# A fused linear attention and feed-forward kernel: one batch's x transposed by DMA instead of TensorE, and the steps of three batches set at other places

## The chip, the cores and the metric

The kernel runs on one core of a Trainium2 chip. The core has five engines, each with its own in-order instruction stream: TensorE (PE in the profile; PEld is its weight load), VectorE (DVE), ScalarE (ACT), GpSimd (POOL) and SyncE (SP). Here SP does nothing but issue DMA transfers; one transfer of the whole program is issued by ACT. The engines wait for each other and for transfers through semaphores. The metric is the device time of one execution in microseconds (us), the median of several runs; lower is better.

## The reference

There are 8 batches of 8 heads with 576 positions and head dimension 64. A linear attention with cosine weights is followed by a feed-forward network over all 4608 tokens of width 512.

```python
r = np.maximum(x, 0.0)
phi = np.concatenate([r * cos_w, r * sin_w], axis=-1)     # 64 -> 128 features, for q and k
kv  = np.einsum('bhsf,bhsd->bhfd', k_p, v)
z   = np.sum(k_p, axis=2)
num = np.einsum('bhsf,bhfd->bhsd', q_p, kv)
den = np.einsum('bhsf,bhf->bhs', q_p, z)[..., None] + 1e-06
x   = (num / den).transpose(0, 2, 1, 3).reshape(B * S, H * D)
h   = x @ w_in                                            # 512 -> 2048
out = np.maximum(0.01 * h, h) @ w_out                     # 2048 -> 512
```

## The kernel before

**Tiling.** Of each batch the first 512 positions form one group of tokens, numbered as the batch, 0 to 7. The 64 positions left over of all eight batches form a ninth group, 8. A group's 512 tokens lie as 128 partitions times J = 4 (`p j` with p outer), so one j is a tile of 128 tokens. Everything that TensorE reads is float16, and it accumulates in float32 in PSUM.

**What one batch b needs, in order.**

- `load_k`, `load_v` and `load_main("q")` (L86, with the small tails of k and v at L96) fetch the inputs as float32. Each of them takes a buffer from the pool `stage`, which has seven.
- `kv_steps` puts `k_tail` and four `k_main` (both halves of phi of k, L226 on DVE, L224 on ACT), two `v_main` and one `v_tail` (casts of v to float16, L232 on ACT or L234 on DVE; `v_tail` is two instructions, one for each half of the partitions), then `kv_all` (L290 for the tails, which come first and read `vtail`; L299 for the main part) and the copy of the result to `kv[b]` (L306, on ACT).
- `q_steps` puts four `q_prep` (phi of q, L226 on DVE) and, after every second of them, one `q_transpose_dma` (L342), a DMA transposition of two tiles of phi(q) from SBUF to SBUF, issued by SP.
- `num(b, j)` (L373) multiplies tile j by `kv[b]`. It uses the pool `ps_n`, a single PSUM buffer. `divide` (L384 to L389, on DVE) divides by the denominator into the tile `xs`.
- x must be transposed into `xT` before the first matrix multiplication. For batches 3 to 8 `out_steps` does it with one `x_transpose_dma` (L354) for all four tiles, issued by SP. For batch 2 `x_transpose(2, j)` does it on TensorE, four transposes for each j into a PSUM tile `ps_xt` (L438), which ACT copies to `xT` (L439). Batches 0 and 1 are worked by steps of their own, which are written out by hand.

**The feed-forward part.** `ffn1(g, m)`, short f1(g,m), is four matmuls of 512 columns (L452). Two neighbouring m share a PSUM tile of a pool with two buffers, and ACT applies the leaky ReLU to the pair (L460). `ffn2(g, i)`, short f2(g,i), is four matmuls too (L475); four of them make one output tile of 128 tokens. `ffn2_out` copies it to one of four buffers `osb` (L234 or L232) and stores it (L489).

**The order.** The program order is written by hand: every engine takes its instructions in the order in which the Python code names them. For the main part there is a list `units` of f1 and f2 steps, each with a position; group g's second product and group g+1's first product share the positions 16g to 16g+16. `ahead` says how many f2 steps of the group come before the mixing starts. `at(pos, f, ...)` puts any other step at a position, and `weave` merges the two lists: a step stands ahead of the first unit whose position is not below its own.

**SP's queue.** All transfers but one stand in SP's single queue, in program order. Each also waits until the transfer eight places before it has landed, because the transfers use eight semaphores in turn. A transfer whose source is not ready holds up everything that stands behind it.

Of the kernel before, what the change touches and what calls it, by code (L numbers as in the profile page):

```python
# [9 lines left out]
dt = mybir.dt  # L10
# [3 lines left out]
P = 128  # L14
J = 4
# [3 lines left out]
def kernel(  # L19
# [14 lines left out]
    nc = tc.nc  # L34
# [8 lines left out]
    NKC = DM // P  # L43
# [28 lines left out]
    def psum(where, shape, dtype, name):  # L72
        p = {"h": ps_h, "o": ps_o, "n": ps_n}[where]
        return p.tile(shape, dtype, name=name, tag="ps_" + where)

    st = {}
    ACT, DVE, POOL = nc.scalar, nc.vector, nc.gpsimd
# [96 lines left out]
    ident = const.tile([P, P], dt.float16, name="ident")  # L174
# [55 lines left out]
    def copy(eng, o, i):  # L230
        if eng is ACT:
            nc.scalar.copy(o, i)  # L232
        else:
            eng.tensor_copy(o, i)  # L234
# [112 lines left out]
    def xT_tile(g):  # L347
        if ("xT", g) not in st:
            st["xT", g] = xtpool.tile([P, J, NKC, P], dt.float16, name="xT")
        return st["xT", g]  # L350
# [80 lines left out]
                ps.rearrange("p c (o t) -> p o c t", o=2),  # L431
            )

    def x_transpose(g, j, where="o"):
        xs = st["xs", g][:, j]
        ps = psum(where, [P, NKC, P], dt.float16, "ps_xt")
        for c in range(NKC):
            nc.tensor.transpose(ps[:, c, :], xs[:, 2 * c : 2 * c + 2, :], ident)  # L438
        nc.scalar.copy(xT_tile(g)[:, j], ps)  # L439

    def ffn1(g, m, lo=0, hi=MAIN, chunks=range(NKC), where="h"):
# [18 lines left out]
    def ffn2(g, i, eng=DVE):  # L462
        tt, part = divmod(i, 4)
        if g == NG - 1 and tt == 3:
            last_tile(*divmod(part, 2))
            return
        if part == 0 and ("ps_o", g, tt) not in st:
            st["ps_o", g, tt] = psum("o", [P, DM], dt.float32, "ps_o")
        ffn2_mm(g, tt, 4 * part, 4 * part + 4)
        if part == 3 and eng is not None:  # L470
            ffn2_out(g, tt, eng)

    def ffn2_mm(g, tt, lo, hi):
        for m in range(lo, hi):
# [5 lines left out]
                stop=(m == NFT - 1),  # L480
            )

    def ffn2_out(g, tt, eng):
        ps = st["ps_o", g, tt]
        osb = opool.tile([P, DM], dt.float32, name="osb", tag="osb")
        if g < B:
            copy(eng, osb, ps)
            rows = out[g * S : g * S + MAIN, :].rearrange("(p j) d -> p j d", j=J)
            nc.sync.dma_start(rows[:, tt, :], osb)  # L489
            return  # L490
        copy(eng, osb, ps)
        for o in range(2):
            r0 = (2 * tt + o) * S + MAIN
            nc.sync.dma_start(out[r0 : r0 + TAIL, :], osb[o * TAIL : (o + 1) * TAIL, :])
# [66 lines left out]
    ps = psum("h", [P, 2, 512], dt.float32, "ps_numh")  # L561
# [44 lines left out]
    def f1(g, m, where="h"):  # L606
        return lambda: ffn1(g, m, where=where)

    def f2(g, i):
        return lambda: ffn2(g, i)  # L610
# [3 lines left out]
    def at(pos, f, *args):  # L614
        steps.append((pos, lambda: f(*args)))
# [22 lines left out]
    ps = psum("n", [P, 2, DM], dt.float32, "ps_o")  # L638
# [16 lines left out]
    v_main(1, 6, 8, ACT)  # L655
    ffn2(0, 15, None)
    ffn2_out(0, 2, ACT)
    ffn2_out(0, 3, ACT)
    ffn2(0, 3, None)
    ffn2_mm(0, 1, 12, 14)  # L660
    kv_half(1, 1, "h")
    ffn2_mm(0, 1, 14, 15)
    ps = psum("h", [P, 2, MAIN], dt.float16, "ps_x")
# [24 lines left out]
    for m in range(6, NFT):  # L688
        units.append((8 + m / 2, f1(1, m)))
    for g in range(1, NG):  # L690
        ahead = {1: 8, 2: 4}.get(g, 0)
        order = [f2(g, i) for i in range(ahead)]
        for i in range(16):
            if g + 1 < NG:
                order.append(f1(g + 1, i))
            if ahead + i < 16:
                order.append(f2(g, ahead + i))
        for n, u in enumerate(order):
            units.append((16 * g + 16 * n / len(order), u))
# [3 lines left out]
    def kv_steps(b, start, step, mm, eng_v, n_act=0):  # L703
        at(start - 0.01, kp_tiles, b)
        at(start, k_tail, b, DVE, DVE)
        for i in range(J):
            at(start + (i + 1) * step, k_main, b, i, ACT if i < n_act else DVE, DVE)
        v0, dv = (start + 1.5 * step, 1) if b > 3 else (start + 3 * step, 0.1)
        at(v0, v_main, b, 0, 4, eng_v)
        at(v0 + dv, v_main, b, 4, 8, eng_v)  # L710
        at(v0 + 2 * dv, v_tail, b, eng_v)
        at(mm, kv_all, b)

    def load_steps(b, pk, pv, pq):
        at(pk, load_k, b)
        at(pv, load_v, b)
        at(pq, load_main, "q", q, b)

    def out_steps(b, start, step, lag):
        for j in range(J):  # L720
            at(start + j * step, num, b, j)
        at(start + (J - 1) * step + lag, x_transpose_dma, b)

    def q_steps(b, start, step, lag):
        for j in range(J):
            at(start + j * step, q_prep, b, j)
            if j % 2:
                at(start + j * step + lag, q_transpose_dma, b, j // 2)

    q_steps(2, 8, 0.4, 0.3)  # L730
    kv_steps(2, 9.7, 0.5, 14, DVE, 2)
    for j in range(J):
        at(14.5 + 1.1 * j, num, 2, j)
        at(15.8 + 1.1 * j, x_transpose, 2, j, "o" if j < 2 else "h")

    load_steps(3, 11, 13, 10)
    q_steps(3, 18, 0.8, 0.8)
    kv_steps(3, 20, 0.7, 24, ACT)
    out_steps(3, 24.5, 1.4, 1)

    load_steps(4, 21.4, 22.5, 21.3)
    kv_steps(4, 28, 1.2, 34, ACT)
    q_steps(4, 30, 0.8, 0.8)
    out_steps(4, 36.8, 2, 1.6)

    for b in range(5, NG):
        base = 16 * (b - 2)
# [40 lines left out]
```

## Time and profile before

| | us |
|---|---|
| median of 3 runs | 294.44 (294.29 to 294.61) |
| the profiled execution | 293.82 |
| its span, first to last instruction | 292.0 |
| TensorE's idle time in the span, all waits that the profile names | 1.2 + 0.5 + 0.2 + 0.2 |

The span is what the profile shows; the execution's time has 1.8 us around it. These groups belong to the stages that the change touches (line, engine and operation, output and input, shapes, count, then busy us and the mean ns of one, then the idle time of the engine before them and what ended it):

```profile
L299 PE MATMUL ps_kv<-vmain,kpm 128*128 128x66 f16 x192 | 7.1, 193 | 0.0
...
out_dram<-osb SPq DMA_DIRECT2D x32, 256.0 KB, 2.5
...
qpT<-qp SPq DMA_TRANSPOSE x14, 4.5
...
xT<-xs SPq DMA_TRANSPOSE x6, 4.6
```

The last three are lines on transfers: destination and source, queue, count, KB of each and the median us from issue to landing. A matmul's duration in such a line is from its start to its modelled end. Successive matmuls overlap, so what one costs is the distance between two starts.

### The profile page before, as it was taken

What the parts mean: (1) busy time and instruction counts of PE and PEld (TensorE: products, weight loads), DVE (VectorE), ACT (ScalarE), POOL (GpSimd) and SP (SyncE); (2) the same over time, 40 slices, a digit from 0 to 9 for tenths busy, and PEclk for the clock granted to TensorE, in tenths of its full rate; (3) what the DMA queues carried; (4) which work ended last, traced back from release to release, by engine and by line L of the source; (5) the groups of instructions that cost most, each with busy time, mean ns of one, the idle gap of its engine ahead of it and who ended that gap; (6) DMA issues with size and microseconds to landing.
All of it is one profiled execution on the core that took longest, in us unless ns stands there. A gap on an engine that the chain in (4) does not pass through costs nothing.

```text
span 292.0 us, 4774 instructions
## 1 busy us (share of the span) xinstructions
PE 286.4 (98%) x1958; PEld 152.7 (52%) x1958; DVE 128.7 (44%) x328; ACT 118.4 (41%) x148; POOL 12.7 (4%) x24
## 2 busy tenths in 40 slices
PE   8999999999999999999999999999999999999995
PEld 3585556555555555455545554555445444444444
DVE  6931687926835816823562356333323310000011
ACT  6865266753544632632263226322222222222200
POOL 2264000000000000000000000000000000000000
PEclk9999999999999999999999999999999999999999
DMA  7999999999999999789584989504691051011133
GB/s 233 348 386 407 325 364 335 315 204 324 212 241 318 229 291 298 166 162 338 164 182 84 296 233 199 91 37 110 160 199 38 36 108 38 36 54 54 39 71 73
DMA packets 87909, 56.93 MB, mean 195 GB/s; under 512 B 55888, under 2 KB 80720, under 8 KB 87504
## 3 DMA queue, kind: packets, MB, share of 16 engines
q1 hardware_dynamic: 87808, 56.57, 71.0%
q8 instruction: 15, 0.25, 0.4%
q10 hardware_dynamic: 80, 0.07, 0.1%
q14 instruction: 6, 0.05, 0.1%
HBM read 36.70 MB, written 9.44 MB: 158 GB/s over the span
## 4 chain that ended last, share of the span: by engine, by line
PE 94%; DMA 2%; SPq 1%; ACT 1%; DVE 1%; issue 0%
PE ps_h L452 43%; PE ps_o L475 41%; PE ps_num L373 3%; PE ps_kv L299 2%; DMA vst<-in_v_dram 2%; PE ps_l L504 1%; SPq L96 1%; PE ps_xth L425 1%; PE ps_qt L363 1%; PE ps_numh L409 1%; SPq L86 1%; PE ps_kv L290 0%; PE ps_idle L166 0%; PE ps_kvh L274 0%; ACT qpT L232 0%; PE ps_xt L438 0%
## 5 line engine op out<-in xcount | busy, mean ns | idle before, releaser
L452 PE MATMUL ps_h<-xT,w 128*128 128x512 f16 (+1 forms) x592 | 142.8, 373 | 0.1
L475 PE MATMUL ps_o<-w,g 128*128 128x512 f16 x560 | 139.5, 379 | 0.0
L460 ACT ACTIVATE g<-ps_h 128x1024 f16<-128x1024 f32 x72 | 73.2, 1023 | 128.8 <-PE ps_h L452 128.8
L452 PEld LDWEIGHTS <-w 128*128 128x128 f16 x592 | 64.4, 114 | 52.3 <-issue 0.2
L475 PEld LDWEIGHTS <-g 128*128 128x128 f16 x560 | 54.2, 98 | 61.4
L234 DVE COPY osb<-ps_o 128x512 f32<-128x512 f32 x31 | 21.4, 690 | 77.1 <-PE ps_o L475 75.3
L384 DVE TENSOR_SCALAR den<-ps_num 128x8 f32<-128x8 f32 x28 | 4.6, 165 | 54.9 <-PE ps_num L373 54.9
L389 DVE TENSOR_TENSOR xs<-ps_num,rden 128x512 f16<-128x512 f32 x28 | 19.4, 691 | 1.2 <-DVE rden L388 0.2
L226 DVE TENSOR_SCALAR kpm<-kst,sin_t 128x512 f16<-128x512 f32 (+1 forms) x40 | 16.6, 429 | 1.1 <-DMA kst<-in_k_dram 1.1
L226 DVE TENSOR_SCALAR qp<-qst,cos_t 128x512 f16<-128x512 f32 (+1 forms) x34 | 15.5, 456 | 2.8 <-DMA qst<-in_q_dram 2.8
L226 DVE TENSOR_SCALAR qp<-qst,sin_t 128x512 f16<-128x512 f32 (+1 forms) x34 | 15.5, 456 | 0.0
L373 PEld LDWEIGHTS <-qpT 128*128 128x128 f16 (+1 forms) x256 | 10.6, 101 | 7.3 <-issue 1.7
L232 ACT CAST vmain<-vst 128x1024 f16<-128x1024 f32 (+1 forms) x14 | 12.5, 920 | 2.4 <-DMA vst<-in_v_dram 2.3
L226 DVE TENSOR_SCALAR kpm<-kst,cos_t 128x512 f16<-128x512 f32 (+1 forms) x29 | 13.1, 453 | 0.3 <-DMA kst<-in_k_dram 0.3
L373 PE MATMUL ps_num<-kv,qpT 128*128 128x66 f16 (+1 forms) x256 | 11.8, 194 | 0.0
L166 PE MATMUL ps_idle<-blank 128*128 128x512 f16 x30 | 9.9, 478 | 1.2 <-DVE blank L161 1.2
L234 DVE CAST w<-w2st 128x1024 f16<-128x1024 f32 (+1 forms) x6 | 5.1, 868 | 11.8 <-DMA w2st<-in_moe_w_out_dram 11.8
L232 ACT COPY qpT<-ps_qt 128x1024 f16<-128x1024 f16 x7 | 7.0, 1012 | 5.7 <-PE ps_qt L363 5.7
L234 POOL CAST w<-w1st 128x1024 f16<-128x1024 f32 (+1 forms) x9 | 8.5, 945 | 3.6 <-DMA w1st<-in_moe_w_in_dram 3.6
L388 DVE RECIPROCAL rden<-den 128x8 f32<-128x8 f32 x36 | 7.3, 203 | 1.2
L299 PE MATMUL ps_kv<-vmain,kpm 128*128 128x66 f16 x192 | 7.1, 193 | 0.0
L299 PEld LDWEIGHTS <-kpm 128*128 128x128 f16 x192 | 6.4, 98 | 0.3
(62 smaller groups left out, 99.7 us busy)
## 6 DMA issues: line engine op xcount, KB each, us to landing
out_dram<-osb SPq DMA_DIRECT2D x32, 256.0 KB, 2.5
qst<-in_q_dram SPq DMA_DIRECT2D x7, 1024.0 KB, 6.8
kst<-in_k_dram SPq DMA_DIRECT2D x6, 1024.0 KB, 9.7
vst<-in_v_dram SPq DMA_DIRECT2D x6, 1024.0 KB, 9.4
w1st<-in_moe_w_in_dram SPq DMA_DIRECT2D x7, 512.0 KB, 10.4
w2st<-in_moe_w_out_dram SPq DMA_DIRECT2D x3, 1024.0 KB, 12.9
kst<-in_k_dram SPq DMA_DIRECT2D x4, 512.0 KB, 6.9
vst<-in_v_dram SPq DMA_DIRECT2D x4, 512.0 KB, 7.9
```

The costliest lines, as they stand in the source:

```text
L166: nc.tensor.matmul(ps, lhsT=blank[:, 0:P], rhs=blank)
L226: eng.tensor_scalar(out=o, in0=i, scalar1=0.0, scalar2=col, op0=ALU.max, op1=ALU.mult)
L232: nc.scalar.copy(o, i)
L234: eng.tensor_copy(o, i)
L299: nc.tensor.matmul(ps[:, h % 2, h // 2], lhsT=kpm[:, h, j, :], rhs=vmain[b % 2][:, h, j, :], start=False, stop=(h >= H - 2 and j == J - 1),)
L373: nc.tensor.matmul(ps[lo:hi, h // 4, (h % 4) * NE : (h % 4 + 1) * NE], lhsT=qpT[:, h, lo:hi], rhs=kv[b][:, h, :],)
L384: nc.vector.tensor_scalar_add(den.rearrange("p (a b) -> p a b", a=2), ps[:, :, D : 4 * NE : NE], 1e-6)
L388: nc.vector.reciprocal(rden, den)
L389: nc.vector.tensor_tensor(out=xs, in0=ps[:, :, 0 : 4 * NE].rearrange("p a (b e) -> p a b e", e=NE)[:, :, :, 0:D], in1=rden.rearrange("p (a ...
L452: nc.tensor.matmul(ps[:, m % 2, lo:hi], lhsT=w1[m // 4, c][0][:, w1[m // 4, c][1], m % 4 : 512 : 4], rhs=xT[:, lo // P : hi // P, c, :], s ...
L460: nc.scalar.activation(st["g", g][:, m - 1 : m + 1, :], ps, AF.Lrelu)
L475: nc.tensor.matmul(st["ps_o", g, tt], lhsT=st["g", g][:, m, tt * P : (tt + 1) * P], rhs=w2[:, m, :], start=(m == 0), stop=(m == NFT - 1),)
```

## The change

There are five edits.

1. `x_transpose` is gone. Batch 2 uses `out_steps(2, 14.4, 0.9, 0.8)`: its four `num` stand 0.9 of a position apart (before 1.1), and its x is transposed by one `x_transpose_dma`. The 16 transposes and four copies leave TensorE and ACT.
2. The four stores of group 0 are not issued where the tiles are copied. They are held in a list and issued at position 9.6, which puts them behind the two q transposes of batch 2 in SP's queue.
3. `ahead` becomes 15 for group 1 (before 8) and 8 for group 2 (before 4), so that group 1's second product stands almost whole before f1(2,0).
4. Batch 3's v (the fourth batch's) is loaded at position 18 (before 13), behind the transposition of batch 2's x. Its casts stand at 24.6, 25.4 and 26.2 (before 22.1, 22.2 and 22.3), and `kv_all(3)` at 27 (before 24).
5. The other steps of batches 3 and 4 stand later; batch 4's `kv_steps` start at 31 (before 28), and its `kv_all` at 36 (before 34).

```diff
-    def x_transpose(g, j, where="o"):
-        xs = st["xs", g][:, j]
-        ps = psum(where, [P, NKC, P], dt.float16, "ps_xt")
-        for c in range(NKC):
-            nc.tensor.transpose(ps[:, c, :], xs[:, 2 * c : 2 * c + 2, :], ident)
-        nc.scalar.copy(xT_tile(g)[:, j], ps)
...
+    held = []
+
+    def store_held():
+        for rows, osb in held:
+            nc.sync.dma_start(rows, osb)
...
-            nc.sync.dma_start(rows[:, tt, :], osb)
+            if g == 0:
+                held.append((rows[:, tt, :], osb))
+            else:
+                nc.sync.dma_start(rows[:, tt, :], osb)
...
-        ahead = {1: 8, 2: 4}.get(g, 0)
+        ahead = {1: 15, 2: 8}.get(g, 0)
...
-        v0, dv = (start + 1.5 * step, 1) if b > 3 else (start + 3 * step, 0.1)
+        v0, dv = (start + 3 * step, 0.1) if eng_v is DVE else (start + 1.5 * step, 1)
+        if b == 3:
+            v0, dv = start + 3.1, 0.8
...
-    for j in range(J):
-        at(14.5 + 1.1 * j, num, 2, j)
-        at(15.8 + 1.1 * j, x_transpose, 2, j, "o" if j < 2 else "h")
-
-    load_steps(3, 11, 13, 10)
-    q_steps(3, 18, 0.8, 0.8)
-    kv_steps(3, 20, 0.7, 24, ACT)
-    out_steps(3, 24.5, 1.4, 1)
-
-    load_steps(4, 21.4, 22.5, 21.3)
-    kv_steps(4, 28, 1.2, 34, ACT)
+    at(9.6, store_held)
+    out_steps(2, 14.4, 0.9, 0.8)
+
+    load_steps(3, 11, 18, 10)
+    q_steps(3, 18.2, 0.8, 0.8)
+    kv_steps(3, 21.5, 0.8, 27, ACT)
+    out_steps(3, 27.5, 1.1, 1)
+
+    load_steps(4, 22.5, 24, 22.4)
     q_steps(4, 30, 0.8, 0.8)
-    out_steps(4, 36.8, 2, 1.6)
+    kv_steps(4, 31, 1, 36, ACT)
+    out_steps(4, 37.5, 1.9, 1.6)
```

In the new order around `kv_all(3)` TensorE has f2(1,0) to f2(1,14), then f1(2,0), f2(1,15), f1(2,1), f1(2,2), and so on to f1(2,5), then `kv_all(3)`. ACT has, after f1(2,1): the leaky ReLU of units 0 and 1, two `v_main`, the leaky ReLU of units 2 and 3, two `v_tail`, the leaky ReLU of units 4 and 5, the copy of kv(3).

## The prediction

> **What bounds the kernel now.** Batches are counted from 0, so "the third batch" is batch 2. f1(g,m) and f2(g,i) are the units of the hand-written order: four 512-column matmuls each. I read the page's busy table first, then its chain of waits, then TensorE's waits and the busy times by stretch.
>
> ```profile
> PE 286.4 (98%) x1958; PEld 152.7 (52%) x1958; DVE 128.7 (44%) x328; ACT 118.4 (41%) x148; POOL 12.7 (4%) x24
> ...
> PE 94%; DMA 2%; SPq 1%; ACT 1%; DVE 1%; issue 0%
> ...
> 60.80:76.80 16.00, 16.00 (x149) 9.21 (x142) 8.80 (x24) 5.83 (x8) 0.00 (x0) 1.00 0.98 272
> 76.80:101.00 24.20, 24.20 (x181) 12.78 (x179) 16.05 (x43) 13.84 (x17) 0.00 (x0) 1.00 1.08 249
> ```
>
> TensorE (PE) is busy 98% of the span and 94% of the chain; in the stretches that the change touches (the last two lines: us, PE busy, count) it has no idle time, at a granted clock of 1.00. So time can be gained only by removing PE work, and any new PE wait is lost in full. The other engines are under 45%, yet each works in order, and that decides below.
>
> The timeline of PE gives the prices (start, us, count):
>
> ```profile
> 65.60 0.42 PE L373 MATMUL ps_num<-kv,qpT 128*128 128x66 f16 x8
> 65.85 0.39 PE L438 MATMUL ps_xt<-ident,xs 128*128 128x128 f16 x4
> 66.08 1.89 PE L475 MATMUL ps_o<-w,g 128*128 128x512 f16 x8
> ...
> 80.20 1.03 PE L475 MATMUL ps_o<-w,g 128*128 128x512 f16 x4
> 81.16 0.30 PE L290 MATMUL ps_kv<-vtail,kpt 64*128 64x66 f16 x8
> 81.39 1.19 PE L299 MATMUL ps_kv<-vmain,kpm 128*128 128x66 f16 x32
> 82.42 1.03 PE L452 MATMUL ps_h<-xT,w 128*128 128x512 f16 x4
> ...
> 92.08 5.34 PE L452 MATMUL ps_h<-xT,w 128*128 128x512 f16 x24
> 97.26 3.62 PE L475 MATMUL ps_o<-w,g 128*128 128x512 f16 x16
> ```
>
> From start to start: a num step 0.255, four x transposes 0.22 to 0.23, a unit 0.863 (24 matmuls in 5.18), and the kv group 1.36 (from 80.20+0.86 to 82.42).
>
> **Removed.** Sixteen transposes on PE at 0.0555: **-0.89 us**. ScalarE (ACT) also loses four 0.58 us copies, off the path.
>
> **The order around kv(3): a new wait.** PE is as before up to num(2,0) at 62.75. Then come three units of f1(1), sixteen of f2(1), f1(2,0) and f1(2,1): 21 units, 18.13, and four nums, 1.02, so f1(2,1) ends at 81.90. Four units later (f1(2,2) to f1(2,5), 3.45) stands kv_all(3), whose first matmuls read both halves of vtail: the second at 85.46. ACT has by its new order, all after f1(2,1): g of units 0/1, two vmain casts, g of 2/3, two vtail casts. The old timeline has all of these back to back:
>
> ```profile
> 77.01 1.02 ACT L460 ACTIVATE g<-ps_h 128x1024 f16<-128x1024 f32 x1 [2.93 <-PE ps_h L452]
> 77.93 1.98 ACT L232 CAST vmain<-vst 128x1024 f16<-128x1024 f32 x2
> 79.81 0.83 ACT L232 CAST vtail<-vtl 64x256 f16<-64x256 f32 x2
> 80.67 1.02 ACT L460 ACTIVATE g<-ps_h 128x1024 f16<-128x1024 f32 x1
> ...
> 99.01 1.02 ACT L460 ACTIVATE g<-ps_h 128x1024 f16<-128x1024 f32 x1
> 99.93 0.82 ACT L232 CAST vtail<-vtl 64x256 f16<-64x256 f32 x2
> ```
>
> g 0.92, two vmain 1.88, g 0.92, two vtail 0.83: 4.55. The first g starts 0.26 after its unit (76.75 to 77.01), at 82.16, so the second vtail is there at 86.71, or 86.73 with the handover. PE waits 86.73 - 85.46 = **+1.27 us**. Before, the units of f1 and f2 alternated here, only one g stood ahead of the tails, and 80.64 came in time for 81.16. Behind the tail casts waits g of 4/5, then the copy of kv(3); both have over 0.7 us to spare in the two-buffer PSUM ring. Bounds of this wait: 1.27 if v is there, nothing if some of these casts proved to be done earlier (rival below); above it only if v lands after 83.1.
>
> **Stores, x and v moved on SP's queue, priced at nothing.** SP issues in order, and each DMA waits for the eighth before it. The two q transposes pass four stores (256 KB each); num(2,0), which PE did not wait for, gets them earlier. The stores free the four output buffers by about 64, and the next copy needs one at 70.3: 6 us of cover. xT(2) is issued behind the store of osb(1,0), which waits for DVE until 70.9: issue 71.3, and 4.4 to 5.5 to landing (the six xT rows) gives 76.8 at most; f1(2,0) needs it at 79.31. Batch 3's v is queued behind that: issue 73.3, a load landing 6.1 to 6.8 after its issue (the q rows at 128.59 and 159.94), 80.1; ACT casts it at 83.08. So 2.5 and 3.0 us cover these, and a loss beyond the cover is one for one. The four nums stand 0.4 us apart beyond the 1.58 us that one divide takes (62.75 to the end of xs at 64.33) before the single ps_num buffer is free.
>
> **The later order of batches 4 and 5: a second wait at the edge.** kv(3) ends at 85.36+1.36+1.27 = 87.99. The three transposes qpT(4), xT(3), qpT(4) now follow each other on SP. The first needs qp(4,1): num(3,3) starts at 87.99 + eight units 6.91 + three nums 0.76 = 95.66, the divide and two 0.39 us halves on DVE end 2.4 later, issue 98.1. The queue before:
>
> ```profile
> 97.74 4.69 SPq L342 DMA_TRANSPOSE qpT<-qp  x2
> 102.52 0.64 SPq L86 DMA_DIRECT2D qst<-in_q_dram  x1
> ...
> 118.49 1.78 SPq L342 DMA_TRANSPOSE qpT<-qp  x1
> 120.38 2.23 SPq L354 DMA_TRANSPOSE xT<-xs  x1
> ```
>
> From the first of two to q 4.78 (0.36 of it a wait for DVE); the third adds the 2.41 between the landings of the lower pair (4.4 and 4.9 after issue). q(5) goes out at 105.2, xT(3) lands at 104.9 against a need at 105.91 (0.98 of cover). In the old trace v's first cast starts 14.51 after q's issue (102.52 to 117.03, with a store between them as now): 119.71. Behind those casts ACT holds g of f1(3,6/7), 1.88 + 1.02 later, 122.65 with the handover; its PSUM buffer is wanted by f1(3,10) at 87.99 + 36 units 31.08 + 8 nums 2.04 + kv 1.36 = 122.47. A wait of about **+0.2 us**. Five q-to-v intervals before (issue of q to landing of v) are 15.4, 14.2, 14.4, 13.1 and 14.3, which bounds it between nothing and 1.2; I take the 14.4, the only one with the store.
>
> The Trainium skill's page "DMA: Bandwidth & Descriptors" (section "Latency and other measured facts") gives a DMA transposition 261 GB/s, which for the 512 KB here is an estimate of 2.0 us. By it the q(5) load would leave 0.8 earlier, the second wait would vanish, and the sum below would be 0.2 less; the trace's 2.41 between two landings disagrees, and I go by the trace.
>
> **Sum.** -0.89 + 1.27 + 0.2 = **+0.58 us**. The profiled execution took 293.82 (span 292.0 and 1.8 around it) and would take 294.4; the median of the runs is 0.62 above it, 294.44, so **295.0** there. Batches 6 to 8 keep their steps and only shift.
>
> **Rivals.** A measurement of this kernel tells 0.2% from no change, 0.59 us: faster is below 293.85, slower above 295.03.
>
> 1. *Faster: kv(3) does not wait* (0.09). It decides at one point: both vtail casts done by 85.46, that is 3.3 us after the first g instead of 4.55. For it: kv(3) never waited before, and ACT is 41% busy. Against: the order above, in which nothing waits for a DMA. With cover for the second wait too, 294.44-0.89 = 293.55.
> 2. *The q(5) chain is later* (0.20). If loads run as at 62.06 (15.4), the second wait is 1.2, and the tail of k(5), on which DVE's queue and the divides of num(4) stand, comes late with it, partly overlapped: 296.0. For it: the DMA engines are near full here. Against: one interval in five.
> 3. *A transposition is late* (0.06). As the one at 53.98, behind stores and loads, with 7.8 instead of 4.5 to landing: xT(3) 2.3 beyond its cover, 297.1. The stores are no longer ahead of it, which speaks against.
> 4. *The first wait is half as long* (0.05), because some of the casts overlap more: 294.2 to 294.6.
>
> The forecast itself has 0.60, at 294.8 to 295.5, of which 0.34 within 0.2% and 0.26 above. So faster 0.09, same 0.34+0.05 = 0.39, slower 0.26+0.20+0.06 = 0.52. The range of 293.9 to 296.3 leaves out rival 1, rival 3 and the end of rival 2.
>
> **What would show it.** PE's waits after: one of about 1.2 to 1.4 us at L290 on ACT near 86, and one on ACT at the f1 line near 122 of 0 to 1.2. ACT's timeline near 82 to 87.5 in the order g, vmain, vmain, g, vtail, vtail without a gap. xT(2) without a waiting matmul. I am wrong if PE passes 86 without a wait, if ACT waits there for vst, or if f1(2,0) or f1(3,0) waits for its xT.

## The result and the profile after

| | median us | runs | profiled execution | its span |
|---|---|---|---|---|
| before | 294.26 | 293.89 to 294.61 (6) | 293.82 | 292.0 |
| after | 296.79 | 296.39 to 298.65 (6) | 296.73 | 295.0 |

The changed kernel takes 1.0098 [1.0069, 1.0127] times as long: slower, by 2.5 us, where the prediction had 295.0 and 293.9 to 296.3. The direction was right and the size was not.

The page of after, first its busy table (busy us, share of the span, instructions), then the shares of the chain that ended last:

```profile
PE 286.5 (97%) x1942; PEld 151.6 (51%) x1942; DVE 128.4 (44%) x328; ACT 116.1 (39%) x144; POOL 12.6 (4%) x24
...
PE 85%; DMA 5%; DVE 3%; ACT 2%; SPq 2%; issue 1%; ACTq 0%; DVEq 0%
```

The 16 transposes and four copies are gone (1958 to 1942, 148 to 144). TensorE's share of the chain fell from 94% to 85%, and transfers have 5% of it (2% before). The busy times by stretch (start and end us, length, then busy us and count for PE, PEld, DVE, ACT and POOL, the granted clock, the DMA engines' busy share, GB/s) show where:

```profile
60.80:76.80 16.00, 16.00 (x137) 8.53 (x136) 9.20 (x24) 3.67 (x4) 0.00 (x0) 1.00 1.00 258
76.80:101.00 24.20, 23.15 (x169) 12.54 (x168) 12.84 (x35) 11.26 (x13) 0.00 (x0) 1.00 1.10 268
101.00:131.00 30.00, 28.89 (x227) 15.37 (x226) 16.30 (x42) 13.65 (x17) 0.00 (x0) 1.00 1.00 239
```

The third column is TensorE: nothing idle up to 76.8, then 1.05 and 1.11 us, where before had none. Before's first two of these lines stand in the prediction; its third is

```profile
101.00:131.00 30.00, 30.00 (x242) 16.36 (x235) 13.84 (x35) 12.07 (x14) 0.00 (x0) 1.00 0.91 227
```

The view of what TensorE waited for names the releasers (engine, output and line, releaser; us in total, times, longest):

```profile
PE ps_kv L290 <- ACT vtail L232: 1.1, 2, 0.8
PE ps_num L373 <- DVE xs L389: 0.8, 1, 0.8
...
PE ps_kv L299 <- DVE kpm L226: 0.2, 1, 0.2
```

The view counts idle time, and a wait costs a little more than that, because matmuls overlap. Measured as the distance from one start to the next beyond the usual pitch, after has these waits past 60 us: 1.29 at `kv_all(3)` (the group and its wait take 2.86 from the last matmul ahead to the first behind, where before's take 1.57; the expectations below count this wait as 1.26), 0.24 at f1(3,0) for xT(3), 0.95 at num(4,3), 0.26 at f1(3,10), 0.32 in `kv_all(5)`. The last four, 1.77 in all, are called the late waits below. Together with the 0.89 removed that is 1.29 + 1.77 - 0.89 = 2.17. The two profiled executions differ by 2.91; 0.49 of the rest stands already at 50.6 us, ahead of the first transfer that the change moves, and 0.25 is in gaps under 0.14 us each (0.13 of it at f1(4,0)), which I do not place.

**The first wait.** TensorE's and then ACT's timeline of after near `kv_all(3)` (start us, us, what; in brackets the idle time before it and its releaser):

```profile
84.34 1.67 PE L445 MATMUL ps_h<-xT,w 128*128 128x512 f16 x7
86.82 0.19 PE L290 MATMUL ps_kv<-vtail,kpt 64*128 64x66 f16 x1 [0.81 <-ACT vtail L232]
87.25 0.28 PE L290 MATMUL ps_kv<-vtail,kpt 64*128 64x66 f16 x7 [0.24 <-ACT vtail L232]
```

```profile
82.66 1.02 ACT L453 ACTIVATE g<-ps_h 128x1024 f16<-128x1024 f32 x1 [15.09 <-PE ps_h L445]
83.58 1.99 ACT L232 CAST vmain<-vst 128x1024 f16<-128x1024 f32 x2
85.46 1.03 ACT L453 ACTIVATE g<-ps_h 128x1024 f16<-128x1024 f32 x1
86.38 0.82 ACT L232 CAST vtail<-vtl 64x256 f16<-64x256 f32 x2
87.22 1.02 ACT L453 ACTIVATE g<-ps_h 128x1024 f16<-128x1024 f32 x1
```

ACT works without a gap from 82.66, in the order of the prediction, and each half of `vtail` releases one part of the group.

**The queue behind.** SP's timeline, first of before, then of after (the second number is how long the issue lasted). It starts with the load of batch 3's v, or with what now stands ahead of it:

```profile
68.35 0.66 SPq L86 DMA_DIRECT2D vst<-in_v_dram  x1
...
75.62 5.82 SPq L342 DMA_TRANSPOSE qpT<-qp  x2
81.96 0.53 SPq L86 DMA_DIRECT2D qst<-in_q_dram  x1
```

```profile
71.40 0.36 SPq L492 DMA_DIRECT2D out_dram<-osb  x1
71.81 3.07 SPq L354 DMA_TRANSPOSE xT<-xs  x1
74.92 0.59 SPq L86 DMA_DIRECT2D vst<-in_v_dram  x1
...
79.31 6.34 SPq L342 DMA_TRANSPOSE qpT<-qp  x2
...
86.65 0.40 SPq L86 DMA_DIRECT2D qst<-in_q_dram  x1
...
98.61 3.40 SPq L342 DMA_TRANSPOSE qpT<-qp  x1
102.11 2.45 SPq L354 DMA_TRANSPOSE xT<-xs  x1
104.66 2.02 SPq L342 DMA_TRANSPOSE qpT<-qp  x1
106.77 0.88 SPq L86 DMA_DIRECT2D qst<-in_q_dram  x1
```

Batch 4's q leaves at 86.65 instead of 81.96. To take out the start, times are counted from the first matmul of `kv_all(2)` (60.63 before, 61.12 after) from here on where "after kv(2)" is said: q(4) leaves 25.5 instead of 21.3 after kv(2), q(5) 45.7 instead of 41.9. The new transposition, the first of the pair behind it and the one at 98.61 take 3.07, 3.75 and 3.40 to issue; in the fifth run below the last of these takes 1.83, with nothing in flight ahead of it. Each of these issues ends when what stands ahead has landed: the store issued at 71.40 lands at 75.09 and the xT issue ends at 74.88; a store lands at 83.16 and the first qpT issue ends at 83.06; a store lands at 102.30 and the issue of 98.61 ends at 102.01.

**What the late queue stops.** DVE's timeline of after, ahead of num(4,3):

```profile
114.46 0.68 DVE L234 COPY osb<-ps_o 128x512 f32<-128x512 f32 x1
118.03 0.35 DVE L226 TENSOR_SCALAR kpt<-ktl,cos_t 128x256 f16<-128x256 f32 x1 [2.89 <-DMA ktl<-in_k_dram]
...
120.14 0.16 DVE L384 TENSOR_SCALAR den<-ps_num 128x8 f32<-128x8 f32 x1
120.33 0.20 DVE L388 RECIPROCAL rden<-den 128x8 f32<-128x8 f32 x1
120.57 0.69 DVE L389 TENSOR_TENSOR xs<-ps_num,rden 128x512 f16<-128x512 f32 x1
```

DVE stands idle for 2.89 us at the head of its order, waiting for the tail of batch 5's k. The divide of num(4,2), whose input TensorE delivered between 116.66 and 117.08, stands six instructions behind, and num(4,3) needs the single `ps_num` buffer that this divide frees at 121.26.

### The profile page after: what moved, and what is told of

The parts are those of the page before. It is cut to its first block, busy times and chain, and to the rows that moved or that the text cites. A ratio compares the mean times of both kernels' runs of the same rounds, so it can differ in the third digit from the quotient of the medians.

```text
span 295.0 us, 4741 instructions
## 1 busy us (share of the span) xinstructions
PE 286.5 (97%) x1942; PEld 151.6 (51%) x1942; DVE 128.4 (44%) x328; ACT 116.1 (39%) x144; POOL 12.6 (4%) x24
## 4 chain that ended last, share of the span: by engine, by line
PE 85%; DMA 5%; DVE 3%; ACT 2%; SPq 2%; issue 1%; ACTq 0%; DVEq 0%
PE ps_o L468 39%; PE ps_h L445 38%; DMA ktl<-in_k_dram 3%; PE ps_kv L299 2%; PE ps_num L373 2%; DMA vst<-in_v_dram 2%; PE ps_l L507 1%; SPq L96 1%; DVE kpm L226 1%; SPq L86 1%; ACT vmain L232 1%; DVE qp L226 1%; PE ps_xth L425 1%; PE ps_qt L363 1%; PE ps_numh L409 1%
## 5 line engine op out<-in xcount | busy, mean ns | idle before, releaser
L468 PE MATMUL ps_o<-w,g 128*128 128x512 f16 x560 | 137.5, 379 | 0.0
```

Source lines behind the costliest of these rows:

```text
L468: nc.tensor.matmul(st["ps_o", g, tt], lhsT=st["g", g][:, m, tt * P : (tt + 1) * P], rhs=w2[:, m, :], start=(m == 0), stop=(m == NFT - 1),)
```

## The experiments

The question was whether the loss is the first wait and some chance waits (then each can be taken away by itself), or the first wait and a queue that is later as a whole. All kernels but the eighth are the changed kernel with the edit shown. Waits are start-to-start excesses, as above.

| run | median us | its before | ratio, 95% interval |
|---|---|---|---|
| e1_vtail_dve | 296.88 | 294.19 | 1.0081 [1.0057, 1.0104] |
| e2_v_early | 297.57 | 294.19 | 1.0112 [1.0087, 1.0136] |
| e3_x_on_pe | 296.70 | 294.19 | 1.0084 [1.0069, 1.0099] |
| e4_no_store0 | 296.24 | 294.19 | 1.0076 [1.0047, 1.0105] |
| e5_x_on_pe_v_early | 296.17 | 294.24 | 1.0055 [1.0035, 1.0074] |
| e6_batch5_later | 295.89 | 294.24 | 1.0060 [1.0040, 1.0080] |
| e7_all_mended | 295.22 | 294.24 | 1.0022 [1.0005, 1.0039] |
| e8_before_extra_t | 296.44 | 294.24 | 1.0069 [1.0046, 1.0092] |
| e9_all_mended_kv4_later | 296.06 | 294.48 | 1.0055 [1.0034, 1.0077] |
| e10_both_undone_vtail_dve | 295.08 | 294.48 | 1.0024 [0.9998, 1.0051] |

### The first wait alone taken away

```diff
-        at(v0 + 2 * dv, v_tail, b, eng_v)
+        at(v0 + 2 * dv, v_tail, b, DVE if b == 3 else eng_v)
```

> Batch 3's two vtail casts go from ScalarE to VectorE; nothing else changes. In the changed kernel's profile TensorE waited 1.26 us at kv(3) and then, summed, 1.77 us at four places between 106 and 127 (xT(3) 0.24, num(4,3) 0.95, f1(3,10) 0.26, kpm(5) 0.32). Theory 'queue' (from 60 to 120 the transfers are one queue that is always full, and the late waits are set by its end, not by TensorE): the wait at kv(3) vanishes, but TensorE then comes to f1(3,0) 1.26 us earlier and waits there or at the next places that much longer; 296.3 to 296.9. Rival 'additive' (each wait is a cost of its own): 295.5, with the four late waits as they were.

Measured: 296.88, no gain. What TensorE waited for in this run:

```profile
PE ps_h L445 <- DMA xT<-xs: 1.5, 2, 1.1
PE ps_num L373 <- DVE xs L389: 1.2, 1, 1.2
...
PE ps_kv L290 <- ACT vtail L232: 0.2, 1, 0.2
```

The wait at `kv_all(3)` is gone: TensorE passes it at 85.9 (the last line is at `kv_all(4)`). But xT(3) now holds up f1(3,0) by 1.26 instead of 0.24, num(4,3) waits 1.36 instead of 0.95, and f1(4,0) waits 0.56 for its xT. A TensorE that is earlier meets a queue that is no earlier: the wait moved and did not go, as the theory 'queue' had it. So the transfers, and not ACT, set this stretch. (The profiled execution, 297.78, is the longest of the four, so its waits may be larger than those of the others.)

### Batch 3's v back at its old place

```diff
-    load_steps(3, 11, 18, 10)
+    load_steps(3, 11, 13, 10)
```

> Batch 3's v is loaded at position 13 again, ahead of the transposition of batch 2's x; nothing else changes. Theory 'queue': the same transfers in another order, so xT(2) lands some 3 us later and f1(2,0) waits 0 to 1.5 us, kv(3) still waits 1.26, the late waits stay or shrink by what f1(2,0) waits; 296.3 to 297.5. Rival 'place of v' (the late waits come from v's load standing behind xT(2)): the four late waits vanish, 295.0 to 295.5.

Measured: 297.57, the slowest, just above the range of the theory 'queue'. With v (1 MB) ahead of it again, xT(2) lands 21.0 after kv(2) instead of 15.8, and f1(2,0) waits 2.31 for it, more than was expected. The wait at `kv_all(3)` stays at 1.29, since ACT's order is the same. The late waits are gone, but TensorE comes to their places some three to four us later here, so that says nothing of the transfers. What TensorE waited for, and its busy times by stretch around that wait:

```profile
PE ps_h L445 <- DMA xT<-xs: 2.1, 1, 2.1
```

```profile
78.00:79.90 1.90, 1.47 (x7) 0.60 (x6) 1.90 (x6) 0.00 (x0) 0.00 (x0) 1.00 1.94 239
79.90:82.30 2.40, 0.69 (x4) 0.38 (x4) 0.14 (x1) 0.00 (x0) 0.00 (x0) 1.00 0.66 165
82.30:85.70 3.40, 3.40 (x10) 1.25 (x9) 1.24 (x3) 0.00 (x0) 0.00 (x0) 0.53 1.08 221
```

So putting v behind the transposition was needed for xT(2): the change trades one late transfer for another. The third line is taken up under the hardware.

### x of batch 2 back on TensorE, v still late

```diff
-    out_steps(2, 14.4, 0.9, 0.8)
+    for j in range(J):
+        at(14.4 + 0.9 * j, num, 2, j)
+        at(16.4 + 0.9 * j, x_transpose, 2, j)
```

with the function `x_transpose` of before put back (its PSUM tile from the pool of f1).

> The changed order in all, but batch 2's x is transposed on TensorE again (16 transposes, 0.89 us, and four copies on ScalarE). Theory 'queue': with one transposition (2.4 us) less in the full queue, the late waits (1.77 us) go; 296.8 + 0.9 - 1.8 = 295.9, with the wait at kv(3) still 1.26. Rival (the late waits come from the later order of batches 4 and 5 alone): they stay, 297.7.

Measured: 296.70, between the two expectations and not to be told from after. The late waits fell from 1.77 to 0.91, and TensorE had its 0.89 of transposes again: `kv_all(3)` stands that much later after kv(2). The gain of 0.86 and the price of 0.89 cancel, as the time says. q(4) left 24.3 after kv(2) instead of 25.5, but batch 5's loads are no earlier: q(5) leaves at 45.7 and the last part of k(5)'s tail lands at 56.9, against 45.7 and 56.8 in after. So the waits are shorter here because TensorE comes later, and taking the transposition alone out of the queue gains nothing that the time shows.

### The stores of group 0 left out

```diff
-        for rows, osb in held:
-            nc.sync.dma_start(rows, osb)
+        held.clear()
```

The 512 tokens of group 0 are not written in this run.

> The four held stores of group 0 are left out (rows 0 to 511 of the output are not written); nothing else changes. Theory 'queue': 1 MB, some 2.8 us, less in the queue ahead of batch 3's q and k, so all later transfers land earlier and the late waits shrink or go; 295.0 to 296.0, kv(3) still 1.26. Rival (SP's wait for the first output of group 1 at 71.4 absorbs it): 296.6 to 296.9, with the late waits as they were.

Measured: 296.24, between the two expectations. The late waits are 1.27 instead of 1.77, and q(4) leaves 25.2 after kv(2) instead of 25.5. 1 MB less ahead in the queue hardly moves what comes later, because SP stands at the store of osb(1,0) for DVE's result until 10.3 after kv(2), as in after, and the lead is lost there. The held stores are a small part of the loss, some 0.5 of the 2.5 us.

### Both moves in the queue undone

The edits of the second and third run together.

> The changed order, with both moves on SP's queue undone: batch 2's x on TensorE (0.89 us) and batch 3's v loaded at position 13. Theory 'drain' (a DMA transposition is issued to its end only when all earlier transfers have landed, so one between two batches of loads empties the queue; and v's load has to stand ahead of the first stores): q(4) is issued some 21.5 us after kv(2) starts, as before (21.3), instead of 25.5; the late waits near 120 to 127 fall under 0.7 us in sum and kv(3)'s 1.26 us stays; 295.5 to 296.0. Rival 'volume' (the queue only has so many transfers to do, whatever their order): as with x on TensorE alone, 296.7, q(4) at 24.3.

Measured: 296.17, just above the range of the theory 'drain'. q(4) leaves 22.6 after kv(2), the late waits are gone, 0.28 is left at f1(4,0), and the 1.29 at `kv_all(3)` stays. SP's timeline at the three transpositions, where v(4) and the stores have all landed before the first:

```profile
99.13 1.83 SPq L342 DMA_TRANSPOSE qpT<-qp  x1
101.05 2.24 SPq L354 DMA_TRANSPOSE xT<-xs  x1
103.39 3.01 SPq L342 DMA_TRANSPOSE qpT<-qp  x1
106.49 0.59 SPq L86 DMA_DIRECT2D qst<-in_q_dram  x1
```

Against after, TensorE does 0.89 more and waits 1.62 less (1.77 at the four places, and 0.15 more at f1(4,0)): -0.73, and the medians differ by 0.62. What batch 2's transposition and v's place cost behind them is thus 1.6 us of waits, more than the 0.89 that they free. As in the third run, TensorE's own 0.89 is one part of this; the other is that the last part of k(5)'s tail lands 0.8 earlier (56.0 after kv(2)), though q(5) leaves at 45.7 here too.

### Batch 5's steps set later

```diff
-    out_steps(4, 37.5, 1.9, 1.6)
+    out_steps(4, 37.5, 1.8, 0.3)
...
-            kv_steps(b, base - 8, 1.2, base - 2, ACT)
+            if b == 5:
+                kv_steps(5, 41.5, 0.9, 46.6, POOL)
+            else:
+                kv_steps(b, base - 8, 1.2, base - 2, POOL)
...
-        q_steps(b, base - 8, 2, 1)
+        q_steps(b, base - 8, 2, 1.6 if b == 5 else 1)
```

> SP's loads stay as in the changed kernel, but the steps that stand on batch 5's loads come later: k_tail(5) and k_main(5) from position 41.5, kv(5) at 46.6, v casts of batches 5 to 7 on GpSimd, xT(4) ahead of the q transposition of batch 5. Theory 'in-order engines behind a late load': TensorE's waits at num(4,3), f1(3,10) and kpm(5), 1.5 us, vanish although the loads land as late as now; kv(3)'s 1.26 and xT(3)'s 0.2 to 0.8 stay; 295.0 to 295.7. Rival 'the loads themselves are late for kv(5)': the waits come back at kv(5) or at f1(4,0), 296.8.

Measured: 295.89, 0.2 above the range of the first theory. With batch 5's k behind the divides of num(4), no wait is left between f1(3,0) and 131 us: the loss there was DVE's order, which the late k turned into a stall. The profiled execution, 296.96, is one of the slower of its eight; in it v(4) and xT(3) landed 1.6 and 1.7 us later than in after, with the same queue up to there, and `kv_all(4)` waited 0.54 and f1(3,0) 1.38.

### All orders mended

The edits of the sixth run, and: v of batches 3 and 4 cast by GpSimd, which is idle here, so that no g waits behind a cast on ACT; xT(3) issued ahead of batch 4's first q transposition.

```diff
-    kv_steps(3, 21.5, 0.8, 27, ACT)
-    out_steps(3, 27.5, 1.1, 1)
+    kv_steps(3, 21.5, 0.8, 27, POOL)
+    out_steps(3, 27.5, 1.1, 0.65)
...
-    kv_steps(4, 31, 1, 36, ACT)
+    kv_steps(4, 31, 1, 36, POOL)
```

> The changed kernel with all of its waits mended in the order alone: v casts of batches 3 to 7 on GpSimd (kv(3) then needs no ScalarE), xT(3) issued ahead of batch 4's first q transposition, and batch 5's steps later as in the run before. If the waits found in the trace are the whole loss, TensorE runs from 61 to the end without a wait and is shorter than before the change by the 16 transposes: 294.2 - 0.9 = 293.3, up to 294.0 with small waits. Rival: GpSimd's casts slow VectorE's or land later than kv(3) needs them, 294.5 to 296.

Measured: 295.22 (293.59 to 296.15 in 11 of the 12 runs, 298.12 in one), above the 294.0 of the theory and still not below before (1.0022 [1.0005, 1.0039]); the profiled execution, 294.05, is one of the short ones. Of what TensorE waits for past 60 us one line is left:

```profile
PE ps_kv L290 <- POOL vtail L234: 0.7, 2, 0.4
```

The wait at `kv_all(3)` and all the late ones are gone; `kv_all(4)` waits for v(4), which lands 39.9 after kv(2) (before 35.5). Of the 2.53 us between the medians of after and before 0.98 are left: some 1.5 came from places and engines of steps that did not fit the later transfers.

### One more transposition in the kernel before

This is the kernel before, with the second q transposition of batch 3 issued twice.

```diff
     q_steps(3, 18, 0.8, 0.8)
+    at(21.25, q_transpose_dma, 3, 1)
```

> The kernel before, with batch 3's second q transposition issued twice (the second copy is read); no other change. Theory 'queue': the one more transposition pushes all later transfers back by about 2.4 us until the queue has slack near 115, and as v(4)'s casts and k(5) were just in time before, TensorE waits near 100 to 104 and 118: 295.2 to 296.8. Rival (the queue has slack there and a transposition is hidden): 294.2.

Measured: 296.44, 2.2 us slower, with nothing added to TensorE. q(4) leaves 23.5 after kv(2) instead of 21.3, and v(4) lands 1.5 later. TensorE's timeline of this run shows the price, and ACT's the reason:

```profile
98.66 2.97 PE L475 MATMUL ps_o<-w,g 128*128 128x512 f16 x13
102.80 0.60 PE L475 MATMUL ps_o<-w,g 128*128 128x512 f16 x2 [1.18 <-ACT g L460]
```

```profile
98.92 1.05 ACT L232 CAST vmain<-vst 128x1024 f16<-128x1024 f32 x1 [2.71 <-DVE kpm L226]
99.87 1.02 ACT L460 ACTIVATE g<-ps_h 128x1024 f16<-128x1024 f32 x1
100.78 1.03 ACT L232 CAST vmain<-vst 128x1024 f16<-128x1024 f32 x1
101.72 1.02 ACT L460 ACTIVATE g<-ps_h 128x1024 f16<-128x1024 f32 x1
```

A cast of v stands between two g on ACT and starts at 98.92 instead of 96.21 (1.5 of it counted from kv(2)), and f2 waits 1.34 for the g behind it. The view names DVE's kpm, which ended at 98.89; v(4) had landed just before, at 98.84, so both held the cast. The queue of before had no 2 us to spare for a transposition even without any other part of the change. How the other 0.9 us of the medians arise is not shown: this profiled execution was 1.18 late already at kv(2), ahead of the added transfer.

### All mended, and `kv_all(4)` later

The seventh run with `kv_steps(4, 31, 1, 37.4, POOL)` and `out_steps(4, 38.4, 1.6, 0.3)`.

> The run that mended all (v casts of batches 3 to 7 on GpSimd, x of batch 3 ahead of its last q transposition, batch 5 later), with kv_all(4) at 37.4 instead of 36 and the four num of batch 4 from 38.4. In the profile of that run TensorE waited only at kv_all(4), 0.52 + 0.51 us for the two halves of vtail. Theory (only TensorE's waits and its own instructions decide): both waits go, no other comes, and the time is that run's 295.22 less 1.0, near 294.2, or 294.24 - 0.89 = 293.35 if that run's spread was these waits too; at most 0.2% faster than before. Rival (the longer DMA queue costs this order something wherever kv_all(4) stands): the wait moves on to num(4,3), to f1(3,0) or to f1(4,0), and the time stays at 295.0 to 295.5.

Measured: 296.06, no gain. Its profile has, among what TensorE waited for:

```profile
PE ps_h L445 <- DMA xT<-xs: 1.8, 1, 1.8
```

`kv_all(4)` no longer waits, and f1(3,0), which now comes sooner, waits for xT(3), then num(4,3) 0.18, `kv_all(5)` 0.60 and a num of batch 5 0.68 follow. The rival was right that the wait moves on, and the time is above its 295.0 to 295.5.

### Both moves undone and the first wait gone

The fifth run with `vtail` of batch 3 cast by DVE, as in the first.

> Both moves in the queue undone (x of batch 2 transposed by TensorE, v of batch 3 loaded early) and vtail(3) cast by VectorE: of the change only the held stores and the later places of the steps are left. Theory (the two causes are the wait at kv_all(3) and the longer queue, nothing else): the 1.26 us at kv_all(3) go, and 296.17 - 1.26 = 294.9; no wait over 0.3 us in the profile after 80. Rival (the later places of the steps cost something by themselves, through SP's queue): the wait at kv_all(3) goes and comes back near num(4,3) or f1(4,0), 295.5 to 296.2.

Measured: 295.08 against 294.9 expected, 1.0024 [0.9998, 1.0051], which cannot be told from before. The busy times by stretch:

```profile
60.80:76.80 16.00, 16.00 (x148) 9.02 (x147) 8.16 (x21) 6.01 (x8) 0.00 (x0) 1.00 1.06 294
76.80:101.00 24.20, 24.20 (x174) 12.94 (x173) 14.61 (x40) 12.24 (x13) 0.00 (x0) 1.00 0.93 232
101.00:131.00 30.00, 29.90 (x234) 15.98 (x233) 16.15 (x41) 12.78 (x17) 0.00 (x0) 1.00 1.04 246
```

TensorE has no idle time in the first two and 0.10 in the third. From the fifth run to this one the excess over before fell from 1.93 to 0.60 (-1.33), near the 1.29 of the first wait. In the first run, with the late queue, the same edit gained nothing. So the two causes together are the loss that can be measured: by the medians 1.3 for the first wait and 0.6, net of the 0.89 freed, for the two moves. The 0.6 alone is within the intervals of after and of the fifth run; what stands beside it is the traces. What else the change has, the held stores and the later places of the steps, is left with the 0.60.

## Why the prediction was wrong

- **Removed, -0.89: right.** The transposes and copies are gone, and in the runs that put the transposes back (third and fifth) `kv_all(3)` stands 0.89 later after kv(2).
- **The wait at `kv_all(3)`, +1.27: right.** It was 1.29, in the order of ACT that was written down, at 86.8 and 87.25 with no gap on ACT. The third and fifth runs keep it; the tenth is 1.33 shorter without it. It could still not be had back by itself, because the queue stood behind it (first run).
- **Stores, x and v moved on SP's queue, "priced at nothing": the step that failed.** The two covers that it named held. xT(2) was issued at 71.81 and landed at 76.92, for a need at 79.81. v(3) was issued at 74.92 and landed at 82.17, later than the 80.1 forecast, for a cast at 83.58. What the step left out is what stands behind: batch 3's two q transpositions went out at 79.31 instead of 75.62, and counted from kv(2) q(4) left 4.2 later than before (25.5 instead of 21.3; 22.6 with both moves undone) and v(4) landed 4.6 later (40.1 instead of 35.5; 36.8 with both undone). So v(4) was still in flight when the three transpositions of the next step began. Undoing both moves takes away 1.6 us of waits, for 0.89 of TensorE's work (fifth run).
- **Three transpositions in a row, then q(5) at 105.2: mis-sized, and here the late queue became a wait.** The first was issued at 98.61, as forecast (98.1, and 0.49 for the start), but q(5) left 8.16 behind it instead of 7.19. The price came from the row at 97.74, which follows another transposition (94.32); v(4) had landed by the end of that one's issue and the last store 0.23 after it, and the first issue at 97.74 took 1.76. At 98.61 v(4) and a store were still in flight, and the issue took 3.40. In the fifth run, with nothing in flight, it took 1.83, and q(5) left 7.36 behind it, near the forecast. xT(3) landed at 106.62 (forecast 104.9), past its cover: 0.24. Not all of q(5)'s delay is the queue's: of the 3.8 us after kv(2) by which it left later than before, the forecast of 105.2 already had 2.7, from the later order of batches 3 and 4.
- **Batch 5's loads: the place that rival 2 named, and dearer than its 296.0.** Rival 2's condition did not come true: from q(5) to v(5) it was 14.6, near the 14.4 of the forecast and not 15.4. The second wait of 0.2 was 0.26; that this size came out is partly luck, since TensorE came to f1(3,10) later by the waits that the sum did not have, and v(5) by q(5)'s delay. But the sum had no term for batch 5's k. Its tail was late, `kpt(5)` held the divides of num(4) on DVE, and num(4,3) waited 0.95, then `kv_all(5)` 0.32. Rival 2 let this be "partly overlapped". The sixth run, which sets batch 5's k behind the divides, has none of these waits.
- **The rule on the rate of a transposition.** The Trainium skill's page "DMA: Bandwidth & Descriptors" (section "Latency and other measured facts") has 261 GB/s where the middle dimension is not contiguous (some 350 to 400 where it is), which is an estimate of 2.0 us for 512 KB. From the end of the issue to the landing it took 2.04 to 2.21 for xT(2) and the ones at 79.31, 98.61 and 102.11, and 1.41 to 4.56, in the median 2.20, for all 21 of after; so as a duration it is about right. Between two landings in a row it was 2.38 to 2.67 for the three pairs from 79 to 109 us, and 1.56 to 3.35 for all pairs of before and after. What the rate leaves out is the time that the issue waits for the transfers ahead.

So the sum came to 0.58 where TensorE's account has 2.17. Of the missing 1.6, 1.5 (0.24 + 0.95 + 0.32) is in work behind the moved transfers, some 35 to 55 us after the new transposition was issued. Between that account and the difference of the medians, 2.53, some 0.4 us stay open. No order tried here came below before: the two that mended the waits stayed at 1.0022 and 1.0055.

## What to carry to other kernels

A transfer that is added to a queue in which the DMA engines are full costs what stands behind it, not only what needs it. List the next three or four loads of the queue, shift each by the added time, and follow the first consumer of each through its engine's order; a cast that stalls at the head of an in-order engine delays whatever stands behind it. Take a transposition's price from a row in which the queue ahead is as full as it will be. When a run moves work back to an engine, that engine also comes later to everything behind, and its waits shrink by that alone; compare when the transfers land before giving them the credit. When a wait is removed and the time does not move, look for the transfer that the next stage waits for: then the queue is the bound, and the order of the matmuls only decides where its lateness shows.

## What the runs showed of the hardware

**A transposition empties the queue.** In before, the issue of 18 of the 20 DMA transpositions ended between 0.31 us ahead of and 0.50 us behind the landing of the last transfer issued before it; in after, of 19 of 21, between 0.49 ahead and 0.64 behind. The other two of each had nothing in flight; their issues took 1.9 and 3.0 us in before, 1.8 and 3.4 in after. Over all, an issue took 1.35 to 5.1 us, where a load's takes 0.4 to 1.1 if no earlier transfer holds it up. Later transfers are issued before the transposition lands (after: q(5) at 106.77, landing of the one ahead 109.00). So by these traces a transposition's issue waits for the transfers before it. With none in flight it still took the 1.8 to 3.4 us above, which may hold waits for other engines.

**The clock dropped after a gap of 2.1 us.** In the second run TensorE was idle from 79.5 to 81.6. From 82.47 eight matmuls stood 0.43 us apart instead of 0.216; the stretch from 82.3 to 85.7 had a granted clock of 0.53. That added about 1.7 us (8 x 0.21) to the wait of 2.3. The ninth run's gap of 1.78 us was followed by a clock of 1.00. That the gap brought the drop about is not shown: the other three executions of the second run had a mean clock of 1.00, and two of the 21 executions of before that go with the last two runs had 0.992 and 0.993, lower than this one's 0.994, from a kernel whose profile has no such gap past 60 us. The Trainium skill's page "TensorE: Matmul & The Clock Gate" (section "What's actually happening") has a drop to half after an idle window of some 3.4 us, a window that runs free of the kernel; the length of the slow stretch, 3.4, agrees, while the gap ahead of it was shorter than that window.
